# Mixing keys and values of two batches in wide matmuls, with the new layout made by DMA through DRAM scratch

## The chip, the cores and the metric

The kernel runs on one core of a Trainium2 chip. The metric is the device time of one execution in microseconds (us), the median of three runs. The engines are called PE (TensorE, the matmuls), DVE (VectorE), ACT (ScalarE), POOL (GpSimd) and SP (SyncE, which here only issues transfers). PE writes to PSUM, eight banks of 2 KB per partition; DVE and ACT copy from there to SBUF.

## The reference

There are B = 4 batches, H = 8 heads, S = 768 rows and D = 64 columns. The rows of a head are 8 blocks of C = 96 rows. A small 8x8 matrix P per batch and head, normalised five times over rows and columns, mixes blocks of keys and values. Each block of queries then attends to its own mixed block, and the result goes through a gated feed-forward layer.

```
for _ in range(5):
    P = exp(P - max(P, -1)); P = P / sum(P, -1); P = P / sum(P, -2)
k_sorted = einsum('bhij,bhjcd->bhicd', P, k_blocks)
v_sorted = einsum('bhij,bhjcd->bhicd', P, v_blocks)
attn = softmax(q_blocks @ k_sorted^T / 8) @ v_sorted       # within one block of 96
x = attn as (B*S, H*D)                                      # 3072 x 512
out = (silu(x @ w_gate) * (x @ w_val)) @ w_out              # d_ff = 1536
```

## The kernel before, in words

Keys and values lie in SBUF in natural form: partition = (head, block), or (batch in the pair, head, block) for batches 2 and 3 together, and per partition 96 rows of 64 columns, in bf16. `rmix` is a block-diagonal matrix of the P's. The one for batches 2 and 3, `rmix["p"]`, is 128 x 128.

**Mixing and turning in one step.** Scores need keys with D on the partitions, and the product with V needs values with the 96 rows of a block on the partitions. A small matmul does both: the natural data is the stationary operand and `rmix` is the moving one, so the output comes out transposed. `kq_chunk` (line 227) does this for keys, one matmul for each row c and each of two half-arrays (128 x 64 stationary, 64 columns moving). A chunk of 16 rows is 32 matmuls into a pair of PSUM banks, which DVE or ACT then copies to the tile `kqt`. For batches 0 and 1 the other half of the same matmuls turns the queries. For batches 2 and 3 both halves are keys, and the queries go another way: POOL casts them by DMA to DRAM scratch `q_scr` (`q_cast`, line 341), and SP brings them back with a transposing DMA (`q_dma`, line 345). `v_pair_chunk` (line 252) is the same for the values of batches 2 and 3, one matmul of 128 columns for each d. It reads `vch`, a copy of the values ordered (d, c), which POOL makes in four steps (`copy_v`, line 114). Its output is copied to `vt`, whose rows hold D values and a one.

**Attention.** A unit is four blocks of two heads. `scores` makes 8 matmuls, `exps` one exponential on ACT, `av` 8 matmuls with `vt`; DVE takes the reciprocal of the sums and multiplies (tile `st`). The turn of `st` into `xt`, the input of the feed-forward layer, is done either by four PE transposes and a DVE copy (`xtr`) or by a transposing DMA from SP (`x_dma`).

**Feed-forward.** There are eight stages ffn(0) to ffn(7), each of 384 rows of x: 12 gate groups and 12 value groups of 4 matmuls of 384 columns, and the output layer of the stage before in three tiles of three parts, 4 matmuls of 512 columns each. Gate goes to PSUM, ACT takes its tanh, DVE combines both to `gs_sb`; value goes to PSUM and DVE multiplies it with `gs_sb` to `h`.

**PSUM.** Gates, values and some output tiles share three banks ("gen"). One bank ("x") is for transposes and other output tiles. Two pairs of banks ("a" and "b") serve scores, av and the mixing chunks in turn.

**Order.** PE and POOL follow the order in which the program is written. `merge` (line 542) places side work among the groups of a stage: each group counts 0.65 and each output part 0.87, and a side item comes behind the first group at which the sum reaches its number. These numbers are about us of feed-forward work, without the side work. DVE, ACT and SP are ordered by a planner that works with estimated times; each queue then runs in order. In this version the stages that matter are:

```
    merge(ffn(2), units(1, range(4, 8), (0.0, 5.5)) + kqs("p", (13.0, 16.2, 19.4))
          + [(13.0, lambda: q_dma(2)), (16.4, lambda: q_dma(3))])
    merge(ffn(3), vs(v_pair_chunk, 8, [1.15 * n for n in range(8)]) + units(2, range(4), (9.8, 14.0)))
```

`units(2, range(4), ...)` in ffn(3) is the first work that needs mixed keys and values of batches 2 and 3. What `units(b, half)` makes is the input of the feed-forward stage behind it.

## Time and profile before

| | |
|---|---|
| median of three runs (lowest to highest) | 250.45 us (250.2 to 250.91) |
| profiled execution: own time, span | 250.3 us, 248.3 us |
| granted clock of PE | 1.0 |
| busy: PE, DVE, ACT, POOL | 237.2, 157.4, 110.2, 52.5 us |
| stage ffn(2): start and end of its PE work | 77.82 to 107.20 us |
| stage ffn(3) | 107.20 to 136.89 us |
| key mixing for batches 2 and 3, PE (64 matmuls each) | at 93.2, 97.7 and 102.2 us |
| value mixing for batches 2 and 3, PE (8 matmuls each) | eight steps, 107.9 to 119.2 us |
| first scores of batch 2 | 121.3 us |
| the two casts of Q, issued by POOL | at 48.3 and 50.4 us |
| the two transposes of Q, issued by SP | at 85.7 and 92.4 us |

The span runs from the first to the last recorded instruction; the execution's own time has some 2 us around it. A matmul's recorded duration overlaps that of the next one, so the cost of a matmul on PE is read from the distance between starts. A line number such as L236 is a line of the kernel before.

### The profile page before, as it was taken

How to read it: one execution, taken by the hardware profiler on the slowest of the kernel's cores; microseconds unless marked ns; L12 is line 12 of the kernel's file. 1: busy time of each engine (PE TensorE's matmuls, PEld its weight loads, DVE VectorE, ACT ScalarE, POOL GpSimd, SP SyncE). 2: the span in 40 equal slices, each digit the busy share in tenths (PEclk: the TensorE clock that was granted, in tenths of full speed). 3: DMA queues.
4: the chain of work that ended last, by engine and by line, in shares of the span. 5: the costliest groups of instructions: out<-in, count | busy, mean ns of one | idle time of the engine just before them, and what ended most of it. 6: DMA issues, size and time to landing. Idle time of an engine off the chain costs nothing.

```text
span 248.3 us, 6023 instructions
## 1 busy us (share of the span) xinstructions
PE 237.2 (96%) x2552; PEld 141.9 (57%) x2552; DVE 157.4 (63%) x332; ACT 110.2 (44%) x188; POOL 52.5 (21%) x47
## 2 busy tenths in 40 slices
PE   5688999999999999999999999999999999999995
PEld 5375566665565556666655655565555565555543
DVE  6777689785665775857657647755764585446700
ACT  3967543454444444445642552354244334232311
POOL 7938459960059300000000000000000000000000
PEclk9999999999999999999999999999999999999999
DMA  5949999999999299010112121112111111100122
GB/s 101 210 85 171 218 186 225 197 227 216 223 162 194 53 187 156 36 42 3 42 44 64 49 70 32 44 45 74 35 43 42 37 57 57 45 18 26 42 83 89
DMA packets 39530, 24.38 MB, mean 98 GB/s; under 512 B 27728, under 2 KB 35664, under 8 KB 38992
## 3 DMA queue, kind: packets, MB, share of 16 engines
q0 software_dynamic: 21328, 14.16, 38.8%
q1 hardware_dynamic: 18176, 9.84, 15.1%
q8 instruction: 20, 0.33, 0.6%
q14 instruction: 6, 0.05, 0.1%
HBM read 28.32 MB, written 7.86 MB: 146 GB/s over the span
## 4 chain that ended last, share of the span: by engine, by line
PE 85%; DVE 6%; ACT 3%; issue 3%; DMA 2%; DVEq 0%; ACTq 0%; POOLq 0%
PE v_ps L375 24%; PE g_ps L357 23%; PE o_ps L392 23%; PE av_ps L306 3%; PE tkq L236 3%; PE qk L279 3%; DMA v<-in_v_dram 2%; PE tv L258 1%; DVE gs_sb L367 1%; PE tv L248 1%; DVE st L312 1%; PE o_ps L408 1%; ACT e_all L292 1%; DVE h L380 1%; PE x_ps L323 1%
## 5 line engine op out<-in xcount | busy, mean ns | idle before, releaser
L367 DVE SCALAR_TENSOR_TENSOR gs_sb<-th_sb,g_ps 128x384 bf16<-128x384 bf16 x96 | 52.8, 550 | 54.1 <-ACT th_sb L365 51.8
L375 PE MATMUL v_ps<-xt,wv_sb 128*128 128x384 bf16 x380 | 77.5, 326 | 0.5 <-issue 0.2
L357 PE MATMUL g_ps<-xt,wg_sb 128*128 128x384 bf16 x376 | 76.5, 325 | 0.0
L365 ACT ACTIVATE th_sb<-g_ps 128x384 bf16<-128x384 f32 x96 | 47.0, 490 | 57.3 <-PE g_ps L357 54.8
L392 PE MATMUL o_ps<-wo_sb,h 128*128 128x512 bf16 x276 | 64.5, 379 | 0.0
L380 DVE SCALAR_TENSOR_TENSOR h<-v_ps,gs_sb 128x384 bf16<-128x384 f32 x96 | 53.3, 555 | 6.5
L375 PEld LDWEIGHTS <-wv_sb 128*128 128x128 bf16 x380 | 35.7, 97 | 24.5 <-issue 1.8
L357 PEld LDWEIGHTS <-wg_sb 128*128 128x128 bf16 x376 | 34.5, 97 | 22.6 <-issue 0.2
L392 PEld LDWEIGHTS <-h 128*128 128x128 bf16 x276 | 26.1, 98 | 28.3 <-DMA wo_sb<-in_moe_w_out_dram 0.3
L397 ACT COPY o_sb<-o_ps 128x512 f32<-128x512 f32 x23 | 13.4, 585 | 48.7 <-PE o_ps L392 48.7
L122 POOL COPY vch<-v 64x1536 bf16<-64x1536 bf16 (+2 forms) x11 | 28.7, 2648 | 20.4 <-DMA v<-in_v_dram 20.4
L292 ACT ACTIVATE e_all<-qk 96x768 bf16<-96x768 f32 x30 | 22.5, 802 | 9.9 <-PE qk L279 9.9
L312 DVE TENSOR_TENSOR st<-av_ps,r_sb 96x512 bf16<-96x512 f32 x32 | 21.7, 679 | 0.2
L306 PEld LDWEIGHTS <-e_all 96*128 96x128 bf16 x256 | 12.2, 98 | 5.0 <-ACT e_all L292 0.9
L306 PE MATMUL av_ps<-vt,e_all 96*128 96x65 bf16 x256 | 13.5, 194 | 0.2 <-ACT e_all L292 0.2
L216 ACT CAST vt<-tv 96x1024 bf16<-96x1024 f32 (+1 forms) x9 | 9.1, 1027 | 3.7 <-PE tv L258 2.6
L310 DVE RECIPROCAL r_sb<-av_ps 96x8 f32<-96x8 f32 x32 | 6.4, 198 | 7.0 <-PE av_ps L306 7.0
L214 DVE CAST vt<-tv 96x1024 bf16<-96x1024 f32 (+1 forms) x9 | 9.8, 1100 | 1.0 <-PE tv L248 1.0
L214 DVE CAST kqt<-tkq 128x1024 bf16<-128x1024 f32 (+1 forms) x7 | 7.4, 1067 | 3.5 <-PE tkq L236 3.4
L236 PE MATMUL tkq<-rmix,kq 128*64 128x64 bf16 x384 | 7.6, 197 | 1.4 <-issue 0.9
L236 PEld LDWEIGHTS <-kq 128*64 128x64 bf16 x384 | 6.7, 113 | 3.0 <-issue 2.9
L216 ACT CAST kqt<-tkq 128x1024 bf16<-128x1024 f32 (+1 forms) x7 | 6.0, 894 | 5.4 <-PE tkq L236 5.4
(77 smaller groups left out, 127.7 us busy)
## 6 DMA issues: line engine op xcount, KB each, us to landing
out_dram<-o_sb SPq DMA_DIRECT2D x23, 256.0 KB, 2.0
v<-in_v_dram POOLq DMA_DIRECT2D x3, 768.0 KB, 19.8
kq<-in_q_dram POOLq DMA_DIRECT2D x2, 768.0 KB, 13.5
wg_sb<-in_moe_w_gate_dram POOLq DMA_DIRECT2D x6, 256.0 KB, 8.2
wv_sb<-in_moe_w_val_dram POOLq DMA_DIRECT2D x6, 256.0 KB, 9.1
wo_sb<-in_moe_w_out_dram POOLq DMA_DIRECT2D x1, 1536.0 KB, 24.4
kp<-in_k_dram POOLq DMA_DIRECT2D x2, 768.0 KB, 15.1
q_scr<-in_q_dram POOLq DMA_DIRECT2D x2, 768.0 KB, 30.1
```

The costliest lines, as they stand in the source:

```text
L122: eng.tensor_copy(dst, src.transpose([0, 2, 1]))
L214: nc.vector.tensor_copy(dst, src)
L236: nc.tensor.matmul(tp[two * D:(two + 1) * D, lc, :], lhsT=kq_tiles[b][:, at + lc, :], rhs=rm[:, two], start=True, stop=True)
L292: nc.scalar.activation(e_all[:, n:n + 2, 0:4 * C], wide[0:C, :, 0:4 * C], AF.Exp, scale=scale)
L306: nc.tensor.matmul(o[:, two, i4, :], lhsT=e[:, i4 * C:i4 * C + 128], rhs=vt[:, 2 * g + two, half * 4 + i4, :], start=True, stop=True)
L312: nc.vector.tensor_tensor(st.rearrange("p i two d -> p two i d"), o[0:C, :, :, 0:D], r_sb.to_broadcast([C, 2, 4, D]), op=ALU.mult)
L357: nc.tensor.matmul(g_ps, lhsT=wg_sb[:, kc, ts(m, 128)], rhs=xt[:, kc, :], start=(kc == 0), stop=(kc == NKC - 1))
L365: nc.scalar.activation(th_sb, g_ps, AF.Tanh, scale=0.5)
L367: nc.vector.scalar_tensor_tensor(gs_sb, th_sb, 1.0, g_ps, op0=ALU.add, op1=ALU.mult)
L375: nc.tensor.matmul(v_ps, lhsT=wv_sb[:, kc, ts(m, 128)], rhs=xt[:, kc, :], start=(kc == 0), stop=(kc == NKC - 1))
L380: nc.vector.scalar_tensor_tensor(h_tiles[n][:, m, :], v_ps, 0.5, gs_tiles.pop(m), op0=ALU.mult, op1=ALU.mult)
L392: nc.tensor.matmul(o_ps, lhsT=h_w[:, m, ts(t3, 128)], rhs=wo_sb[:, m, :], start=(m == 0), stop=(m == NFC - 1))
```

## The change

Batches 2 and 3 no longer mix and turn in one step. `nat_chunk` takes `rmix["p"]` as the stationary operand and 512 columns of the natural keys or values as the moving one. Twelve such matmuls make all mixed keys of both batches, and twelve all mixed values, still in natural form. Each chunk of 1024 columns is copied to SBUF, keys to a tile `kmix`, values into `vch`.

The new layout is made by DMA. For keys, POOL stores each batch to `k_scr`, with rows (block, c) and columns (head, d), in pieces of 64 elements; SP then loads it with a transposing DMA, as it does the queries (`k_dma`). For values, `v_relay` stores a third of the rows c of all 128 partitions to `v_scr` and loads them back with c on the partitions, one load for each batch, in pieces of 64 elements; both come from POOL. Values need `vch` in the order (d, c) no longer, so the four POOL copies of the pair go.

The side work of ffn(2) and ffn(3) is arranged anew: the keys are mixed first in ffn(2), then the second half of batch 1's attention runs, with the values' mixing in between; ffn(3) has only transfers and the attention of batch 2. The second half of batch 1 turns its result by PE and DVE, as the first half does, and no longer by transposing DMAs. `kqt_tile("q")` is asked for ahead of the tile for keys.

```diff
+    k_scr = [dram.tile([S, H * D], BF16, name=f"k_scr{b}") for b in range(2, B)]
+    v_scr = dram.tile([128, C, D], BF16, name="v_scr")
...
-    def v_pair_chunk(pair, at, n, eng, tag):
...
+    mixed = {}
+
+    def nat_chunk(what, at, eng, tag):
+        src = (kq_tiles["p"] if what == "k" else v_tiles[1]).rearrange("p c d -> p (c d)")
+        if what not in mixed:
+            mixed[what] = (natp.tile([128, C * D], BF16, name="kmix", tag="nat") if what == "k"
+                           else vch[:, 0:C * D])
+        tp = pair_tile("tn", tag)
+        for part in range(2):
+            nc.tensor.matmul(tp[:, part * 512:(part + 1) * 512],
+                             lhsT=rmix["p"].rearrange("p u h i -> p (u h i)"),
+                             rhs=src[:, at + part * 512:at + (part + 1) * 512], start=True, stop=True)
+        drain(eng, mixed[what][:, at:at + 1024], tp)
+
+    def k_out(b):
+        nc.gpsimd.dma_start(
+            out=k_scr[b - 2].rearrange("(i c) (h d) -> h i c d", c=C, d=D),
+            in_=mixed["k"][(b - 2) * R:(b - 1) * R].rearrange("p (c d) -> p c d", d=D))
+
+    def k_dma(b):
+        dst = kqt_tile("p")[:, (b - 2) * GI * C:(b - 1) * GI * C]
+        nc.sync.dma_start_transpose(out=dst.rearrange("p (g s) -> p g s", g=H2), in_=k_scr[b - 2])
+
+    def v_relay(c0, c1):
+        nc.gpsimd.dma_start(out=v_scr[:, c0:c1],
+                            in_=mixed["v"].rearrange("p (c d) -> p c d", d=D)[:, c0:c1])
+        for u in range(2):
+            nc.gpsimd.dma_start(out=vt_tile(1)[c0:c1, u, :, 0:D],
+                                in_=v_scr[u * R:(u + 1) * R, c0:c1].rearrange("n c d -> c n d"))
...
-                if b == 0 or b == 1 and u < H2:
+                if b < 2:
                     todo.append((at + t, lambda w=w, tag=tag: av(b, w, tag)))
                     todo.append((at + t + 3.1, lambda w=w: drain("v", *xtr(b, w))))
...
-    for s in range(4):
-        copy_v(nc.gpsimd, 1, both, s)
-    nc.vector.memset(kqt_tile("p")[:, 2 * GI * C:], 0.0)
-    merge(ffn(2), units(1, range(4, 8), (0.0, 5.5)) + kqs("p", (13.0, 16.2, 19.4))
-          + [(13.0, lambda: q_dma(2)), (16.4, lambda: q_dma(3))])
-    merge(ffn(3), vs(v_pair_chunk, 8, [1.15 * n for n in range(8)]) + units(2, range(4), (9.8, 14.0)))
+    def nats(what, ats, engs):
+        return [(at, lambda m=m: nat_chunk(what, m * 1024, engs[m], "ba"[m % 2])) for m, at in enumerate(ats)]
+
+    kqt_tile("q")
+    merge(ffn(2), nats("k", (0.0, 1.2, 2.4, 3.6, 4.8, 6.0), "vssvss")
+          + [(6.1, lambda: (k_out(2), k_out(3)))] + units(1, range(4, 8), (7.0, 13.3))
+          + nats("v", (11.7, 12.0, 16.8, 18.2, 19.0, 20.0), "svssvs")
+          + [(12.1, lambda: v_relay(0, 32)), (18.3, lambda: v_relay(32, 64)), (20.1, lambda: v_relay(64, 96))]
+          + [(13.0, lambda: q_dma(2)), (22.0, lambda: (nc.vector.memset(kqt_tile("p")[:, 2 * GI * C:], 0.0), k_dma(2)))])
+    merge(ffn(3), [(1.0, lambda: q_dma(3)), (6.0, lambda: k_dma(3))] + units(2, range(4), (11.0, 15.5)))
```

## The prediction

> **What bounds the kernel now.** I read the engine totals and the 40 slices first, to learn which engine has no slack and whether transfers are short where the change lies:
>
> ```profile
> span 248.3 us, 6023 instructions
> ...
> PE 237.2 (96%) x2552; PEld 141.9 (57%) x2552; DVE 157.4 (63%) x332; ACT 110.2 (44%) x188; POOL 52.5 (21%) x47
> ...
> DMA  5949999999999299010112121112111111100122
> ...
> PE 85%; DVE 6%; ACT 3%; issue 3%; DMA 2%; DVEq 0%; ACTq 0%; POOLq 0%
> ```
>
> PE (TensorE) is busy nearly throughout and carries 85% of the chain that ended last. The transfers are heavy in slices 0 to 12 and 14 to 15 (one slice is 6.2 us) and light behind. Next, the busy time of each engine in the two stages that the diff rewrites, ffn(2) and ffn(3):
>
> ```profile
> 77.82:107.20 29.38, 29.38 (x389) 17.52 (x388) 19.25 (x35) 13.45 (x22) 4.73 (x2) 1.00 0.73 109
> 107.20:136.89 29.69, 29.54 (x261) 18.09 (x260) 19.96 (x36) 14.77 (x23) 0.00 (x0) 1.00 0.14 41
> ```
>
> The columns are length, then PE, weight loads, DVE, ACT, POOL, clock, DMA share, GB/s. PE is full, DVE has a third free, ACT half. So a removed PE step is worth its spacing in the chain, as long as DVE and ACT return the PSUM banks in time. The spacings come from the chain, in order of time (start, us, what):
>
> ```profile
> 76.95 0.17 PE x_ps L323 x4
> ...
> 92.60 0.65 PE v_ps L375 x4
> 93.25 1.13 PE tkq L236 x64
> 94.38 2.70 PE o_ps L392 x12
> ...
> 98.86 0.76 PE v_ps L375 x4
> ...
> 104.78 2.59 PE o_ps L392 x12
> ...
> 108.02 0.45 PE tv L258 x8
> ...
> 123.05 0.50 ACT th_sb L365
> 123.56 0.56 DVE gs_sb L367
> ...
> 126.57 0.70 DVE st L312
> ```
>
> The reader should see two things. The small matmuls are cheap: 64 of them take 1.13 us, 18 ns each, although each is recorded at 197 ns. And the few places where the chain leaves PE are all near the exponentials: a tanh that stood behind two of them, and the normalised tile `st`. Last, the transfers that resemble the new ones (issuing queue, count, size, median us to landing):
>
> ```profile
> q_scr<-in_q_dram POOLq DMA_DIRECT2D x2, 768.0 KB, 30.1
> xt<-st SPq DMA_TRANSPOSE x20, 2.3
> kqtq<-q_scr SPq DMA_TRANSPOSE x2, 7.0
> ```
>
> **What the Trainium skill says.** "TensorE: Matmul & The Clock Gate", Step-by-step: back-to-back matmuls of 512 columns follow each other about every 216 ns. The trace agrees: 12 in 2.59 us is 0.216. "DMA: Bandwidth & Descriptors", Anatomy of one DMA (SWDGE): a transfer from POOL costs about 2 us plus its bytes; the trace shows no such transfer alone, but SP's stores land in 2.0. The same page, Why a DMA increments its semaphore by 16: a transfer runs on as many engines, up to 16, as divide the slowest dimension of both sides. The store of the mixed keys has heads (8) outermost, so I expect 8 engines; no row of before has such a shape. The same page, Two DMAs through the same engine are not ordered: a read of scratch must wait for the write's completion, so each relay is two trips in series. The trace of before has no such pair at the place of need.
>
> **The change, on PE.** Removed: 3 key steps of 64 matmuls, 3 x 1.13 = 3.39, and what each costs the group behind it (2.70 for 2.59, 0.76 for 0.65), 3 x 0.11 = 0.33; 8 value steps of 8 matmuls, 8 x 0.45 = 3.6. Together 7.3 us. Added: 24 matmuls of 512 columns, 24 x 0.216 = 5.2; and the second half of batch 1 is turned by PE again, 4 groups x 0.175 (the x_ps row) = 0.7. Together 5.9. Net on PE: -1.4 us.
>
> The two stages hold 0.7 us of PE waits now: 0.13 in ffn(2), 0.55 in ffn(3), found by adding the parts (0.65 a gate or value, 0.864 an output part, 0.55 a score pair, 0.26 an av, and the steps above) and comparing with 29.38 and 29.69. If they went and none came, PE would gain 2.1. That is the most the change can give.
>
> **On DVE and ACT.** Removed: 7 copies out of PSUM on each (DVE 1.22, ACT 1.01 to 1.19). Added: 12 of the same 128x1024 size, 4 on DVE, 8 on ACT, taken at the same 1.2 and 1.0 since only the output's stride changes; and 4 copies of turned tiles on DVE (0.35 each). The total falls, but all of it now lies in ffn(2): DVE 19.25 - 3 x 1.22 + 4 x 1.2 + 4 x 0.35 = 21.8 us in a stage of some 32. The margin is in the groups of four gates and values (5.2 us of PE, 8 x 0.555 = 4.4 of DVE), where it is thin. I laid the new order out and followed the banks (three for gate and value, pairs a and b):
> - Gates 0 to 3 with key steps 0 to 4: two ACT copies stand ahead of a tanh each, and each bank returns 0.1 to 0.2 us before its use. Wait 0.1.
> - Gates 4 to 7: the score pair moves from behind a gate to right behind an output group. ACT then has the output copy (0.585) and two exponentials (1.50) ahead of the next tanh. Where before has exponentials ahead of a tanh (123.05 above), PE lost 0.24; with the output copy I take 0.43. Then value step 1 needs pair a back from the second av: DVE owes 6 gate/value operations (3.3), two normalisations (1.76) and that step's copy before the next score pair, and starts late. I take 0.45.
> - Gates 8 to 11: two value steps follow an av or a copy on the same pair within 1.3 to 1.6 us. Wait 0.25.
> - ffn(3): the first score pair is better placed (that tanh goes first), the second again follows an output group: 0.43, and 0.25 behind it.
>
> Sum 1.9 us; if ACT takes the tanh ahead of the second exponential, some 0.9. The first follows what ACT did at 121.65, two exponentials in a row. The gain of 2.1 against waits of 1.9 leaves -0.2 us.
>
> **Moved or hidden steps.** POOL's four reorderings of V (11.2 us, at 71 to 82) go; nobody waited for them, worth 0. The 4 transposes by SP for batch 1 go (2.3 us to landing, not needed until ffn(3)), worth 0 beside the PE cost above; SP's queue gets lighter. The last transpose for ffn(4) is closer: its av now stands 3.9 us before that stage, plus 0.5 until the fourth weight block needs it. Before took 1.55 from av to issue and 2.3 to landing. Slack 0.5, cost 0; uncovered, up to 1 us.
>
> Keys: the six copies end at about 88. Two stores of 6144 pieces of 128 B follow. The casts of Q, of as many pieces, ended at about 81 and took some 5.7 us each (69.5 to 81 for two); POOL issued each in 3.2. Bounds: 5 us, or 11 each on 8 engines. Landed by 100 to 113. SP's transpose of batch 2 takes 7.0, so 107 to 120, and batch 2's scores start at 121.6 (layout 120.3 and waits). The 7.0-us transpose of batch 3 has until ffn(5). Behind the waiting transposes on SP stand output stores, one per 9 us with three buffers: no wait.
> Values: the third relay can start at 108.5. Its write (512 KB, some 4.6 us with the fixed part) ends at 113; two reads of 2048 pieces of 128 B, into rows of 130 B, are issued in about 1 us each and take 1.3 to 4 us each plus 2: landed at 118 to 124. The first av is at 124. POOL waits on each write with only the next relay behind it. I take these as hidden; the cover is 1 to 9 us.
>
> Buffers: Q^T now takes the tile of batch 0, free at the start of ffn(2), so its first transpose (85.7 before) can start sooner; K^T takes batch 1's, free after the score pair at 97. The 32-column fill before K^T is one DVE memset (0.1). Worth 0.
>
> Span 248.3 - 0.2 = 248.1. The profiled run took 250.3, 2.0 around its span and 0.15 below the median of 250.45; on the median's scale, 250.2.
>
> **Rivals.** (A, forecast) PE's saving is given back in waits for PSUM banks: 250.2, own range 249.5 to 251.
> (B) The saving comes through: tanh goes first and copies fit in DVE's idle time. Speaking for it: DVE idles over 2 us in each output group, and eight value copies in ffn(3) now cost PE nothing. Waits 0.5: -1.6, 248.8. Against it: the third of DVE that is free lies mostly in those output groups.
> (C) Slower: the relays are late at batch 2's first av. Decides once a relay takes more than 15.5 us from its last copy (108.5) to landing (124). If small pieces at odd rows and three transposes at once make it 18, PE stops 2.5 us: 252.7. For it: the Q casts were 30 us from issue to landing in a full queue. Against: the queue is light from 100 on, at 46 GB/s in the last third of ffn(2).
> (D) The waits of A come to twice the size: 3.8 - 2.1 = +1.7, 252.1.
>
> **Numbers.** A 0.52, B 0.25, C 0.13, D 0.10. A measurement of this kernel can't tell less than about 0.3% (0.75 us) from no change. Faster than 249.7: nearly all of B and a fifth of A, 0.34. Slower than 251.2: C, most of D and a little of A, 0.24. The same: 0.42. The range 248.7 to 252.3 leaves out the better half of B and most of C; it is the span of the unknown waits (0.4 to 3.9).
>
> **What would show it.** PE: 24 matmuls of `tn` spaced 0.216, stage ffn(2) at 32.0 to 33 us, ffn(3) at 26 to 27. A shows as value or gate groups spaced by more than 0.65 near score pairs, with DVE or ACT in the chain there; B as none of these; C as the first score pair or av of batch 2 waiting for a DMA. It fails if the wide matmuls are not spaced 0.216, or the planner orders ACT or SP otherwise.

## The result: slower by 16%, and the profile after

| | before | after |
|---|---|---|
| median on one chip, four runs each (lowest to highest) | 250.68 us (250.2 to 251.84) | 291.87 us (289.0 to 293.11) |
| ratio after / before, 95% interval | | 1.1619 [1.1522, 1.1716] |
| profiled execution: own time, span | 250.3, 248.3 us | 289.0, 287.2 us |
| stage ffn(2) | 77.82 to 107.20 | 77.62 to 110.82 |

Here and below, a ratio leaves out the executions in a slower state of the chip, while a median and a range in brackets take in all of them. The forecast of 250.2 was wrong, and its range too. What came is the rival that was given 0.13, the late relay, at fifteen times its size. The page of the kernel after, totals and slices (one slice is 7.2 us):

```profile
span 287.2 us, 5583 instructions
...
PE 238.0 (83%) x2311; PEld 139.2 (48%) x2336; DVE 155.9 (54%) x333; ACT 110.5 (38%) x189; POOL 57.2 (20%) x54
...
PE   5889999999999999930000599999999999999995
...
PEclk9999999999999999995555599999999999999999
DMA  6979999999994758869595612211112012100102
...
PE 53%; DMA 31%; DVE 5%; POOL 5%; issue 4%; ACT 1%; POOLq 0%; DVEq 0%; ACTq 0%
```

PE is as busy in all as before (238.0 against 237.2 us). There is one hole, slices 18 to 22, and DMA now carries 31% of the chain that ended last, where it carried 2%. The waits of the kernel after name the hole (engine, what waits, for what: total, times, longest):

```profile
PE av_ps L328 <- DMA vt<-v_scr: 36.5, 1, 36.5
```

One wait, 36.5 us, at batch 2's first av. The rest of the span's growth of 38.9 us is small: PE's timeline of the kernel after shows that PE comes back at half clock,

```profile
161.14 0.60 PE L328 MATMUL av_ps<-vt,e_all 96*128 96x65 bf16 x8 [36.51 <-DMA vt<-v_scr]
161.96 3.19 PE L414 MATMUL o_ps<-wo_sb,h 128*128 128x512 bf16 x7 [0.22 <-issue]
164.95 0.65 PE L328 MATMUL av_ps<-vt,e_all 96*128 96x65 bf16 x8
```

seven matmuls of 512 columns in the 2.99 us between two starts, where 7 x 0.216 is 1.5: 1.5 us more. The steps around them are slowed too. Stage ffn(3) takes 64.89 us (110.82 to 175.71), so 28.35 without the wait; in e15 below, where no transfer is late, it takes 26.04. These 2.3 us are nearly all of the rest. The Trainium skill ("TensorE: Matmul & The Clock Gate", Part 1: The HAM clock gate) says that after it has been idle PE runs at half its clock for about the first 3.4 us of work, and that this varies from run to run. The trace shows the half clock too, but for longer, some 4.5 us: that follows from the mean granted clock of 0.54 in the 4.86 us from 161.14 on (the columns are those of the windows in the prediction; the clock stands third from the end).

```profile
161.14:166.00 4.86, 4.64 (x26) 2.34 (x28) 1.23 (x4) 0.00 (x0) 0.00 (x0) 0.54 0.23 30
```

The prediction priced a wait for its length alone. Where the 36.5 us come from is in POOL's timeline of the kernel after (start, length of the issue, instruction, idle before and its releaser):

```profile
88.72 3.85 POOL L269 DMA_DIRECT2D k_scr<-kmix  x1 [34.61 <-ACT kmix L218]
108.45 3.83 POOL L269 DMA_DIRECT2D k_scr<-kmix  x1 [15.88 <-DVE vch L216]
112.20 0.67 POOL L278 DMA_DIRECT2D v_scr<-vch  x1
129.29 2.15 POOL L281 DMA_DIRECT2D vt<-v_scr  x2 [16.42 <-DMA v_scr<-vch]
131.42 0.57 POOL L278 DMA_DIRECT2D v_scr<-vch  x1
142.21 2.11 POOL L281 DMA_DIRECT2D vt<-v_scr  x2 [10.21 <-DMA v_scr<-vch]
144.31 0.57 POOL L278 DMA_DIRECT2D v_scr<-vch  x1
153.83 2.11 POOL L281 DMA_DIRECT2D vt<-v_scr  x2 [8.95 <-DMA v_scr<-vch]
```

Two stores of keys, then three relays, each a write and two reads. The second store comes out of POOL only at 108.45, when the first has landed (it takes some 19 us). The first write of values stands behind it, so it leaves at 112.2, although the second copy that it needs, on DVE, ended at 97.9. Then each write is waited for before its reads, and each later write stands behind the reads before it: 16.4, 10.2 and 9.0 us. The last read lands at 161.0; the av is ready at 124.6.

What a write waits for in that time can be seen in the trace's records of single packets of 4 KB, which no view here shows; the length of a packet tells which transfer it belongs to. From 145 to 150, behind the third write's issue, packets of about 1 us are under way, sixteen at a time, as in the third relay's reads alone (157 to 161). The write's own packets, most of them of 0.16 us, come at 151 and 152. So most of that wait is the reads issued just ahead of the write on POOL's queue. In the same way the packets of the first write come at 125 and 126, behind those of the second store.

The sizes, from the list of transfers of the kernel after (queue, count, size, median us to landing):

```profile
k_scr<-kmix POOLq DMA_DIRECT2D x2, 768.0 KB, 19.2
v_scr<-vch POOLq DMA_DIRECT2D x3, 512.0 KB, 10.5
vt<-v_scr POOLq DMA_DIRECT2D x6, 256.0 KB, 9.0
kqtp<-k_scr SPq DMA_TRANSPOSE x2, 7.6
```

The prediction had 5 to 11 for the first row, 4.6 for the second, 3.3 to 6 for the third.

### The profile page after: what moved, and what is told of

It reads as the page before. It is cut to its first block, busy times and chain, and to the rows that moved or that the text cites. A ratio compares the mean times of both kernels' runs of the same rounds, so it can differ in the third digit from the quotient of the medians.

```text
span 287.2 us, 5583 instructions
## 1 busy us (share of the span) xinstructions
PE 238.0 (83%) x2311; PEld 139.2 (48%) x2336; DVE 155.9 (54%) x333; ACT 110.5 (38%) x189; POOL 57.2 (20%) x54
## 4 chain that ended last, share of the span: by engine, by line
PE 53%; DMA 31%; DVE 5%; POOL 5%; issue 4%; ACT 1%; POOLq 0%; DVEq 0%; ACTq 0%
PE o_ps L414 19%; PE v_ps L397 14%; PE g_ps L379 13%; DMA v_scr<-vch 13%; DMA wo_sb<-in_moe_w_out_dram 8%; DMA kq<-in_k_dram 4%; DMA wv_sb<-in_moe_w_val_dram 4%; DMA vt<-v_scr 2%; PE av_ps L328 2%; DVE gs_sb L389 2%; PE qk L301 2%; DVE h L402 1%; POOL k_scr L269 1%; POOL wg_sb L111 1%; PE tn L263 1%
## 5 line engine op out<-in xcount | busy, mean ns | idle before, releaser
L414 PE MATMUL o_ps<-wo_sb,h 128*128 128x512 bf16 x257 | 63.3, 386 | 1.9 <-DVE h L402 0.4
L419 ACT COPY o_sb<-o_ps 128x512 f32<-128x512 f32 x23 | 13.5, 587 | 92.5 <-PE o_ps L414 92.5
L328 PE MATMUL av_ps<-vt,e_all 96*128 96x65 bf16 x256 | 13.9, 197 | 36.9 <-DMA vt<-v_scr 36.5
L414 PEld LDWEIGHTS <-h 128*128 128x128 bf16 x276 | 26.8, 99 | 30.8 <-issue 2.4
L124 POOL COPY vch<-v 64x1536 bf16<-64x1536 bf16 (+1 forms) x7 | 17.5, 2539 | 2.6 <-DMA v<-in_v_dram 2.6
L269 POOL DMA_DIRECT2D k_scr<-kmix x2 | 7.7, 3841 | 50.5 <-ACT kmix L218 34.6
L281 POOL DMA_DIRECT2D vt<-v_scr x6 | 6.4, 1067 | 35.6 <-DMA v_scr<-vch 35.6
## 6 DMA issues: line engine op xcount, KB each, us to landing
kp<-in_k_dram POOLq DMA_DIRECT2D x2, 768.0 KB, 14.7
```

Of the source, the lines that this page charges most:

```text
L124: eng.tensor_copy(dst, src.transpose([0, 2, 1]))
L328: nc.tensor.matmul(o[:, two, i4, :], lhsT=e[:, i4 * C:i4 * C + 128], rhs=vt[:, 2 * g + two, half * 4 + i4, :], start=True, stop=True)
L414: nc.tensor.matmul(o_ps, lhsT=h_w[:, m, ts(t3, 128)], rhs=wo_sb[:, m, :], start=(m == 0), stop=(m == NFC - 1))
L419: nc.scalar.copy(o_sb, o_ps)
```

## The experiments

In the order in which they were run. A kernel's times stand beside runs of the kernel before on the same chip (median 251.04 to 251.39 us). Where a time is of one run only, what is read from it is its profile, or a difference of several us.

### One half of the change alone

Keys by the new way, values by the old small matmuls (e1_k_only), and the reverse (e2_v_only). At this point two theories stood: that the stores of keys, spread over few engines and ahead in POOL's queue, hold the relays up; and that the relays are late by themselves.

```diff
# e1_k_only: values mixed by small matmuls in ffn(3), as before
-          + nats("v", (11.7, 12.0, 16.8, 18.2, 19.0, 20.0), "svssvs")
-          + [(12.1, lambda: v_relay(0, 32)), (18.3, lambda: v_relay(32, 64)), (20.1, lambda: v_relay(64, 96))]
-    merge(ffn(3), [(1.0, lambda: q_dma(3)), (6.0, lambda: k_dma(3))] + units(2, range(4), (11.0, 15.5)))
+    merge(ffn(3), [(1.0, lambda: q_dma(3)), (6.0, lambda: k_dma(3))] + vs(v_pair_chunk, 8, [1.15 * n for n in range(8)])
+          + units(2, range(4), (9.8, 14.0)))
```
```diff
# e2_v_only: keys mixed by small matmuls at the start of ffn(2)
-    merge(ffn(2), nats("k", (0.0, 1.2, 2.4, 3.6, 4.8, 6.0), "vssvss")
-          + [(6.1, lambda: (k_out(2), k_out(3)))] + units(1, range(4, 8), (7.0, 13.3))
+    merge(ffn(2), kqs("p", (0.0, 2.4, 4.8)) + units(1, range(4, 8), (7.0, 13.3))
...
-    merge(ffn(3), [(1.0, lambda: q_dma(3)), (6.0, lambda: k_dma(3))] + units(2, range(4), (11.0, 15.5)))
+    merge(ffn(3), [(1.0, lambda: q_dma(3))] + units(2, range(4), (11.0, 15.5)))
```

> Keys mixed wide and relaid by DMA as in the change; values as in the kernel before (POOL's four reorderings, eight small-matmul steps in ffn(3)). Theory 1 (the value relays, pushed back behind the key stores on POOL, are the whole loss): the first store lands near 108, the transpose at 116, the first scores of batch 2 need it at 121, so PE waits for no transfer. On PE: -3.7 for the key steps, +2.6 for twelve wide matmuls, +0.7 for the turns by PE, so about -0.4 plus up to 1 us of bank waits: 249.5 to 251.5. Rival (the key path alone is late as well): PE waits at the first scores, 254 or more.

> Values mixed wide and relayed as in the change; keys by small matmuls as in the kernel before (in the place of the wide key steps), so no key stores and no key transposes. Theory 1 in its plain form (only the key stores in front hold the relays up): the first relay's write starts near 97, the third relay has landed by 124, PE waits for nothing: 250 to 252. Rival, theory 2 (three relays in series are too long by themselves, some 12 us each as they show when they run one after the other at 131 to 161): the third lands near 130 to 133, PE waits 6 to 9 us at the first av of batch 2: 256 to 260.

e1: 255.47 us (254.71 to 258.66), ratio 1.0177 [1.0107, 1.0247]. Two stages take 29.92 and 30.75 us where before took 29.38 and 29.69. No score waits for keys, so the time is in the rival's range without the rival's wait. In these stages the trace names two larger waits of PE, 1.0 and 0.5 us, and the chain leads from both to SP: the transpose of batch 3's keys is issued at 128.99 and the four transposes of x queue behind it. That is 1.6 us of the 4.9 by which this profile's span is longer than before's. Another 2.1 lie ahead of ffn(2), which starts at 79.93 here, with waits of 0.65 and 1.35 us for weights at 41.9 and 44.1; the last 1.2 lie behind and were not traced. POOL's timeline of e1 has nothing but the two stores:

```profile
91.04 3.84 POOL L279 DMA_DIRECT2D k_scr<-kmix  x1 [6.24 <-ACT kmix L218]
110.40 3.83 POOL L279 DMA_DIRECT2D k_scr<-kmix  x1 [15.52 <-issue]
```

The second store waits 15.5 us with nothing ahead of it on POOL but the first.

e2: 271.2 us. Without any store of keys PE still waits 18.1 us for `vt`. So the stores are not all of it: both expectations were under. The second write and SP's second transpose of Q took some 17 us each in the same stretch of time, where a write alone took 4 (POOL's and SP's timelines of e2):

```profile
103.79 2.13 POOL L281 DMA_DIRECT2D vt<-v_scr  x2 [3.83 <-DMA v_scr<-vch]
106.83 0.57 POOL L278 DMA_DIRECT2D v_scr<-vch  x1 [0.91 <-ACT vch L218]
124.28 2.10 POOL L281 DMA_DIRECT2D vt<-v_scr  x2 [16.88 <-DMA v_scr<-vch]
```
```profile
104.56 17.41 SPq L369 DMA_TRANSPOSE kqtq<-q_scr  x1
```

By the packet records it is again the reads ahead of the write, those of the first relay, that share the engines with the transpose: from 106 to 121 the packets on POOL's queue take up to 4.6 us each, and some hundred of 0.16 us, the write's, follow at 122 and 123.

### The stores off POOL's queue, or over more engines

```diff
# e3_k_from_sp
-        nc.gpsimd.dma_start(
+        nc.sync.dma_start(
             out=k_scr[b - 2].rearrange("(i c) (h d) -> h i c d", c=C, d=D),
```
```diff
# e4_k_64_rows: 64 partitions outermost, same pieces of 128 B
-            out=k_scr[b - 2].rearrange("(i c) (h d) -> h i c d", c=C, d=D),
+            out=k_scr[b - 2].rearrange("s e -> (s e)").rearrange("(c p d) -> p c d", c=C, d=D),
```

> The changed kernel with the two key stores issued from SP and not from POOL; nothing else. Theory 1: POOL is free when the first values are copied, the first relay starts near 97 and not at 112, and what remains is theory 2's length of the relays beside the stores: PE waits 10 to 22 us and not 36.5, time 264 to 276. Rival (POOL isn't held up, the 16 DMA engines are short): the relays are as late as before, 285 to 292.

> The changed kernel with another order in the key scratch: the outermost dimension of the store is the 64 partitions on both sides, the pieces are 128 B as before (rows 8 KB apart). The keys of batches 2 and 3 that come back are in a wrong order, the work is the same. If the number of DMA engines (8 heads outermost, so 8 of 16) makes the store slow and fills POOL's queue: the store takes 10 us or less in place of 19, the second is issued right behind the first and not when it has landed, the first relay starts near 97, time 262 to 276. Rival (pieces of 128 B into DRAM are slow whatever the shape): the store takes 15 us or more and the time stays at 283 to 292.

e3: 283.0 us. The first write leaves at 99.83 instead of 112.20, so the block on POOL was real. But the lateness went to SP's queue: PE waits 17.1 us for the keys at the scores, 5.3 behind an output copy on ACT whose buffer waits for an output store (SP's queue again), and 3.4 for `vt`. e4: 280.36 us, PE waits 25.3 us for `vt`; both stores leave POOL in a row, in 4.37 us, and take 14.7 us to landing each. Both times lie between the two ranges expected: the places were right and the gains too small. The windows while the stores ran (length, then PE, weight loads, DVE, ACT, POOL, clock, DMA share, GB/s), e3 and then e4:

```profile
91.00:96.00 5.00, 4.72 (x41) 2.88 (x40) 3.37 (x9) 2.48 (x5) 0.00 (x0) 1.00 0.46 65
```
```profile
96.00:101.00 5.00, 4.68 (x45) 2.56 (x44) 4.55 (x11) 1.92 (x4) 0.32 (x1) 1.00 0.99 112
```

With 8 heads outermost the stores move 65 GB/s, with 64 partitions outermost 112. The share of 0.46 looks like half of the engines, but it belongs to the stores issued by SP. In the kernel after, where POOL issues the same store, the window shows

```profile
92.50:105.00 12.50, 12.05 (x103) 6.82 (x104) 9.79 (x21) 6.28 (x10) 0.07 (x1) 1.00 0.70 59
```

a share of 0.70 at 59 GB/s, so the share alone doesn't count engines. The packet records do: in the kernel after eight packets of 4 KB are under way at a time (the median from 94 to 104; nine at most), in e4 sixteen, and they take 0.56 and 0.54 us each. Nor is the cause how far apart the pieces lie in DRAM: 1 KB apart in the kernel after, but 8 KB in e4 and 256 B in e13 below, whose store also has sixteen packets under way. That is the prediction's count of engines, with its price: in the kernel after, 6144 pieces on 8 engines are 768 for each, in about 14.5 us (92.5 to 107), 19 ns a piece. Yet each of these two cures alone gave back only 9 to 12 us: the relays stayed slow.

### Pieces made large

Here I formed a third theory: pieces of 128 B are the cause, because together they are more work than the DMA engines can do before the first av. Large pieces for all (e5_all_large), for keys alone (e6_keys_large), for the reads of values alone (e7_values_large):

```diff
# keys (e5, e6): a partition's row as one piece, in the wrong order
-            out=k_scr[b - 2].rearrange("(i c) (h d) -> h i c d", c=C, d=D),
-            in_=mixed["k"][(b - 2) * R:(b - 1) * R].rearrange("p (c d) -> p c d", d=D))
+        nc.gpsimd.dma_start(out=k_scr[b - 2].rearrange("s e -> (s e)").rearrange("(p f) -> p f", p=R),
+                            in_=mixed["k"][(b - 2) * R:(b - 1) * R])
# reads of values (e5, e7): 4 KB pieces, the column of ones overwritten
-            nc.gpsimd.dma_start(out=vt_tile(1)[c0:c1, u, :, 0:D],
-                                in_=v_scr[u * R:(u + 1) * R, c0:c1].rearrange("n c d -> c n d"))
+            nc.gpsimd.dma_start(out=vt_tile(1)[c0:c1, u].rearrange("c n e -> c (n e)")[:, 0:R * D].rearrange("c (two f) -> c two f", two=2),
+                                in_=v_scr[u * R:(u + 1) * R, c0:c1].rearrange("(p two) c d -> p two (c d)", two=2))
```

> The changed kernel with the same transfers, bytes and waits, but no small pieces: the key stores write 12 KB rows, the relay's reads move 4 KB pieces. The keys and values that come back are in a wrong order and the ones in the value tile are overwritten. Theory 3 (pieces of 128 B are the cause: about 18 to 23 ns each on a DMA engine, 24576 of them, together more engine time than there is before batch 2's first av): no wait for a transfer, stage ffn(2) 32 to 33.5 us, 249.5 to 253. Rival (two trips in series, three relays one behind the other, whatever the pieces): PE waits 5 us or more at the first av, 256 and up.

> Only the key stores write 12 KB rows (the keys come back in a wrong order); the value relays are those of the change. Theory 3: both stores have landed by 97 and no longer hold POOL's queue; the relays alone take some 36 us from 97 to 133, PE waits 8 to 12 us at the first av, 259 to 263. Rival (the relays also lose to the key and query transposes on SP, as in the kernel with new values only, where a transpose took 17 us to issue): PE waits 15 us or more, 266 to 272.

> Only the relay's reads move 4 KB pieces (values in a wrong order, ones overwritten); the key stores are those of the change. The second key store is still queued only when the first has landed, near 108, and the first relay's write stands behind it until 127. Then each relay is short, some 7 us: the third has landed near 146, PE waits 17 to 24 us, 270 to 278. If the relays' reads were the larger part of the loss, the wait would be under 12 us.

e5: 259.71 us (257.65 to 260.96), ratio 1.0337 [1.0259, 1.0415], PE waits 5.8 us for `vt`. That is in the rival's range (a wait of 5 us or more), so pieces are not the whole cause. e7: 275.55 us, as expected, PE waits 21.9. e6: 277.66 us, above both of its expectations, PE waits 24.9. POOL's timeline of e6:

```profile
98.71 0.56 POOL L277 DMA_DIRECT2D v_scr<-vch  x1 [8.97 <-issue]
103.44 2.15 POOL L280 DMA_DIRECT2D vt<-v_scr  x2 [4.17 <-DMA v_scr<-vch]
106.20 0.57 POOL L277 DMA_DIRECT2D v_scr<-vch  x1 [0.61 <-ACT vch L218]
130.44 2.11 POOL L280 DMA_DIRECT2D vt<-v_scr  x2 [23.67 <-DMA v_scr<-vch]
```

The first write leaves 13 us earlier than in the kernel after and lands in 4. The second then takes 24: ahead of it stand the first relay's small reads, and beside them run both transposes of keys, which are no longer held back by the stores. Time taken from one place came back in another. Small pieces are the main price (36.5 us of waiting against 5.8), but no part of them alone. So the third theory was widened: what counts is the sum of what the DMA engines have to do before the first av, and the order of POOL's queue decides which part of it stands ahead.

### The row of 130 bytes

```diff
# e8_rows_160: rows of the value tile 160 B apart, the same pieces
-            t = vtp.tile([C, 2, H * NB, D + 1], BF16, name=f"vt{pair}", tag="vt")
+            t = vtp.tile([C, 2, H * NB, D + 16], BF16, name=f"vt{pair}", tag="vt")[:, :, :, 0:D + 1]
```

> The changed kernel with rows of the value tile 160 B apart and not 130 B, so that every piece of 128 B starts at a multiple of 32 B. If the odd start makes the relay's reads slow: the last two reads land in 5 us or less and not in 7.2, and the time falls by 4 to 8 us. Rival (the number of pieces counts, not where they start): 7 us again, and 286 to 293.

281.06 us; PE waits 28.0 us instead of 36.5. The reads' median falls from 9.0 to 5.3 us, with nothing changed but where a row starts:

```profile
vt<-v_scr POOLq DMA_DIRECT2D x6, 256.0 KB, 5.3
```

The wait fell by 8.5 us, where 4 to 8 of the time were expected. The waits for the second and third write fell as well, from 10.2 and 9.0 us to 6.9 and 5.0, though nothing of the writes was changed: they stand behind the reads. The prediction mentioned "rows of 130 B" and gave them no price.

### One cure after the other

The next three test theory 3, as widened, by taking work from ahead of the first av. e9_all_large_late is e5 with batch 3's store and transpose of keys, which nobody needs before ffn(5), moved to ffn(4). e10_rows_late does the same with small pieces and the wide rows of e8. e12_rows_late_64 adds the store of e4.

```diff
# e9, e10, e12
-          + [(6.1, lambda: (k_out(2), k_out(3)))] + units(1, range(4, 8), (7.0, 13.3))
+          + [(6.1, lambda: k_out(2))] + units(1, range(4, 8), (7.0, 13.3))
...
-    merge(ffn(3), [(1.0, lambda: q_dma(3)), (6.0, lambda: k_dma(3))] + units(2, range(4), (11.0, 15.5)))
-    merge(ffn(4), units(2, range(4, 8), (0.0, 8.0)))
+    merge(ffn(3), [(1.0, lambda: q_dma(3))] + units(2, range(4), (11.0, 15.5)))
+    merge(ffn(4), units(2, range(4, 8), (0.0, 8.0)) + [(0.5, lambda: k_out(3)), (1.0, lambda: k_dma(3))])
```

> The run with all transfers in large pieces (keys in the wrong order, the column of ones overwritten, a tiny extra fill), and batch 3's store and transpose of keys moved from ffn(2)/ffn(3) to ffn(4), behind the value relays. Theory 3 (the sum of what the DMA engines have to do before the first av decides, and the order of POOL's queue decides what of it stands ahead): ahead of the first av are now one store of keys, three transposes and three relays; the relays land some 4 to 6 us earlier than in the run with all transfers large, PE waits 0 to 2 us for vt, and what is left is the change on PE, DVE and ACT alone: 250.5 to 253, ffn(2) at 32.5 to 33.5. Rival (the relays need their own time in series whatever is beside them, and a relay of large pieces takes 10 us): PE still waits 4 us or more, 256 to 260.

> The kernel after with rows of the value tile 160 B apart, and batch 3's store and transpose of keys moved to ffn(4), behind the relays; all pieces still 128 B; nothing left out. Theory 3: the first write is issued at about 103 instead of 112, since no second store blocks POOL, and batch 3's transpose no longer lies beside the relays; of the 28 us that the run with the wide rows waited, 9 go with the store and a few with the transpose: PE waits 13 to 19 us for vt, time 264 to 272. Rival (the relays' own small reads alone are what is late, and the store ahead of them only fills time in which they'd wait for one another): PE waits 22 us or more, 274 to 282.

> As the run with wide rows and the late store, and the one store of keys that is left has 64 partitions outermost (pieces still 128 B, keys in the wrong order), so that it spreads over all 16 engines: it lands some 7 us earlier. Theory 3: the relays start at 100 to 101 and PE waits 8 to 15 us, 259 to 267, 2 to 6 us below the run with 8 engines. Rival (after the first store is through, nothing of it is left on the path: the third value copy at 108 and the relays in series behind it decide): within 2 us of the run with 8 engines.

e9: 251.31 us (249.84 to 254.47, 20 runs) against 251.09, ratio 1.0011 [0.9987, 1.0036]; no wait for a transfer; theory 3 held and its rival fell. e10: 271.37 us. PE waits 8.1 us for `vt`, and 7.9 for `xt` at the next stage, whose transposes now run beside batch 3's late store: 16.0 in all; the 13 to 19 us expected were for `vt` alone. The time is in the expected range. e12: 250.42 us in one run, below both expectations; no wait for a transfer at all. The direction is theory 3's, the size neither theory's. POOL's timelines, e10 and then e12, show why the store's engines were worth so much:

```profile
99.62 0.57 POOL L278 DMA_DIRECT2D v_scr<-vch  x1 [5.92 <-issue]
110.96 2.14 POOL L281 DMA_DIRECT2D vt<-v_scr  x2 [10.77 <-DMA v_scr<-vch]
...
128.48 2.11 POOL L281 DMA_DIRECT2D vt<-v_scr  x2 [5.00 <-DMA v_scr<-vch]
```
```profile
98.60 0.59 POOL L278 DMA_DIRECT2D v_scr<-vch  x1 [7.59 <-issue]
102.83 2.12 POOL L281 DMA_DIRECT2D vt<-v_scr  x2 [3.64 <-DMA v_scr<-vch]
...
119.60 2.11 POOL L281 DMA_DIRECT2D vt<-v_scr  x2 [5.22 <-DMA v_scr<-vch]
```

POOL's wait for the first write is 10.8 us behind the rest of the 8-engine store and 3.6 without it. That 7 us, and 1 us of earlier start, go through the series of relays: the last reads leave 8.9 us earlier, just in time, and the late `xt` goes with them. So the wait falls in steps, 36.5 (after), 28.0 (wide rows), 16.0 (late store), 0 (16 engines). No single cause owns it; the order in which they are taken away sets the share that each seems to have.

### The whole change with its transfers off the path

e12's keys are in the wrong order. e13_heads_apart puts them right: the mixed keys leave the matmul ordered (half of the head pair, head pair, block), and a store then has one even stride over 32 partitions. It also puts the second and third write ahead of their reads.

```diff
+    rmix_k = const.tile([128, 128], BF16, name="rmix_k")
...
-    k_scr = [dram.tile([S, H * D], BF16, name=f"k_scr{b}") for b in range(2, B)]
+    k_scr = [dram.tile([H2, S, 2 * D], BF16, name=f"k_scr{b}") for b in range(2, B)]
...
+                for u in range(2):
+                    nc.vector.tensor_copy(rmix_k[:, u * R:(u + 1) * R].rearrange("p (e g i) -> p e g i", e=2, i=NB),
+                                          rmix["p"][:, u].rearrange("p (g e) i -> p e g i", e=2))
...
+        for e in range(2):
+            nc.gpsimd.dma_start(
+                out=k_scr[b - 2].rearrange("g (i c) (e d) -> e (g i) c d", c=C, e=2)[e],
+                in_=mixed["k"][lo + e * R // 2:lo + (e + 1) * R // 2].rearrange("p (c d) -> p c d", d=D))
...
-        nc.sync.dma_start_transpose(out=dst.rearrange("p (g s) -> p g s", g=H2), in_=k_scr[b - 2])
+        nc.sync.dma_start_transpose(out=dst, in_=k_scr[b - 2].rearrange("g s x -> (g s) x"))
```

e14_fewer_bank_waits is e13 with five places of the PE order and of the copies' engines changed, each at a PE wait for a PSUM bank:

```diff
-    merge(ffn(2), nats("k", (0.0, 1.2, 2.4, 3.6, 4.8, 6.0), "vssvss")
-          + [(6.1, lambda: k_out(2))] + units(1, range(4, 8), (7.0, 13.3))
-          + nats("v", (11.7, 12.0, 16.8, 18.2, 19.0, 20.0), "svssvs")
+    merge(ffn(2), nats("k", (0.0, 1.2, 2.4, 3.6, 4.8, 5.1), "vssssv")
+          + [(6.1, lambda: k_out(2))] + units(1, range(4, 8), (7.0, 13.3), (0.1, 0.0))
+          + nats("v", (11.7, 12.5, 16.8, 18.2, 19.0, 20.0), "svssvs")
...
-    merge(ffn(3), [(1.0, lambda: q_dma(3))] + units(2, range(4), (11.0, 15.5)))
+    merge(ffn(3), [(1.0, lambda: q_dma(3))] + units(2, range(4), (11.0, 15.5), (0.0, 0.8)))
```

(The added pair of numbers moves a score pair forward by so much.)

> A whole kernel with the transfers rearranged: rows of the value tile 160 B apart; batch 3's keys stored and transposed in ffn(4); the mixed keys leave the matmul ordered (half of the head pair, head pair, block) instead of (head, block), by a permuted copy of the mixing matrix, so that two stores of 32 partitions each have one even stride outermost and can spread over 16 engines with the keys in the right order; the second and third write of values stand ahead of the second and third read in POOL's queue. Theory 3: as with the rows 160 B apart, the late store and 64 partitions outermost (250.4): no wait for a transfer at the first av, the stages ffn(2) and ffn(3) together at 59.3 to 59.8 us, and the time within 0.4% of before, 249.8 to 251.8, since the saving of PE is used up by waits for PSUM banks. Rival (32 partitions in a store are as slow as 8 outermost dimensions): the first store takes 18 us again, PE waits 5 us or more, 256 to 265.

> The run before in this call, with five places in the order changed and nothing else: the sixth key step stands ahead of the first output part instead of behind it; the fourth key copy goes to ACT and the sixth to DVE; two score pairs stand ahead of the last output part of their stage instead of behind it; the second value step and its write come 0.65 us later. Each is at one of the four PE waits of 0.25 to 0.43 us seen in ffn(2) and ffn(3), together 1.3. Theory A of the prediction (what PE saves is given back in waits for PSUM banks): ffn(2) and ffn(3) get shorter by 0.6 to 1.3 us, 249.2 to 250.2, 0.2 to 0.5% below the run before. Rival (the waits only move to the next bank, since DVE and ACT are what is short): the same within 0.2%.

e13: 259.2 us (258.59 to 263.75), ratio 1.0305 [1.028, 1.033]; 249.8 to 251.8 was expected. No wait at the first av, and ffn(2) with ffn(3) take 59.23 us, but a new wait stands at batch 3's first scores. PE's timeline of e13:

```profile
153.61 0.26 PE L310 MATMUL qk<-kqtq,kqtp 64*128 64x96 bf16 x2 [5.75 <-DMA kqtp<-k_scr]
```

and SP's:

```profile
142.21 3.31 SPq L369 DMA_TRANSPOSE xt<-st  x2
...
147.88 3.59 SPq L282 DMA_TRANSPOSE kqtp<-k_scr  x1
```

The keys had left POOL at 117.5 to 120; the planner put their transpose behind two of x, which wait for PE's own work.

e14: 257.4 us, ratio 1.0232 [1.0194, 1.0271]. Two edits took away the waits of 0.43 and 0.30 us (first output part, first value group behind the exponentials) and left nothing in their place. The others made new ones, 0.90 and 0.75, where 0.32 and 0.25 had been: a score pair now stood where its bank was still being copied. ffn(2) and ffn(3) together took 59.31, no less than in e13, so theory A's claim for this run fell and its rival's words fit: the waits moved. The whole-kernel difference to e13 is the shorter wait for batch 3's keys (3.5 us).

Two runs for these two points. In e15_sp_in_order SP's queue follows the program, with the keys' transpose ahead of the four of x; e16_two_waits is e15 with only the two good edits of e14.

```diff
# e15, against e13
-    man = tc.manual_schedule(engines={ET.PE, ET.Pool})
+    man = tc.manual_schedule(engines={ET.PE, ET.Pool, ET.SP})
...
-          + [(13.0, lambda: q_dma(2)), (22.0, lambda: (nc.vector.memset(kqt_tile("p")[:, 2 * GI * C:], 0.0), k_dma(2)))])
-    merge(ffn(3), [(1.0, lambda: q_dma(3))] + units(2, range(4), (11.0, 15.5)))
+          + [(0.1, lambda: q_dma(2)), (4.0, lambda: q_dma(3)), (14.1, lambda: (nc.vector.memset(kqt_tile("p")[:, 2 * GI * C:], 0.0), k_dma(2)))])
+    merge(ffn(3), units(2, range(4), (11.0, 15.5)))
```
```diff
# e16, against e15
-    merge(ffn(2), nats("k", (0.0, 1.2, 2.4, 3.6, 4.8, 6.0), "vssvss")
-          + [(6.1, lambda: k_out(2))] + units(1, range(4, 8), (7.0, 13.3))
+    merge(ffn(2), nats("k", (0.0, 1.2, 2.4, 3.6, 4.8, 5.1), "vssssv")
+          + [(6.1, lambda: k_out(2))] + units(1, range(4, 8), (7.0, 13.3), (0.1, 0.0))
```

> As the run with the heads apart, but SP's queue follows the order of the program from ffn(0) on, with the transposes of Q at the start of ffn(2) and the one of batch 3's keys at the start of ffn(4), ahead of the four transposes of x there instead of behind two of them. If the 5.8 us that PE waited for batch 3's keys at 147.4 were a matter of place in SP's queue (that transpose was issued at 147.9, 30 us after its data had been stored), the wait goes, no other transfer is late, and the time is 250.3 to 252, within 0.4% of before. If the transpose is late for its data or for the DMA engines, PE still waits 3 us or more, 254 or more.

> The run beside it in this call, with two of the five edits for the bank waits kept: the sixth key step ahead of the first output part (fourth key copy on ACT, sixth on DVE), and batch 1's score pair ahead of the last output part of the first half of ffn(2). These took away waits of 0.43 and 0.30 us without leaving new ones; the other edits had put 0.90 and 0.75 in the place of 0.32 and 0.25. Theory A: ffn(2) and ffn(3) together 0.5 to 0.8 us shorter than in the run beside it, 0.2 to 0.3% less time, and at or just below the kernel before: 249.8 to 251.2. Rival (each wait taken away comes back one bank later): no shorter than the run beside it.

e15: 251.61 us (249.89 to 253.79, 22 runs) against 251.29, ratio 1.0011 [0.999, 1.0032]. The wait for keys is gone, so it was a place in SP's queue. e16: 249.85 us (248.31 to 251.56, 22 runs), ratio 0.9944 [0.9923, 0.9965]: faster than the kernel before, by 0.6%, measured on one chip, and the only version here that is shown to beat both. The two stages in windows, e15 and then e16 (columns as before):

```profile
77.47:110.64 33.17, 31.88 (x233) 17.46 (x236) 21.51 (x41) 17.99 (x27) 6.45 (x7) 1.00 1.05 188
110.64:136.68 26.04, 25.63 (x194) 14.50 (x196) 16.08 (x32) 10.30 (x19) 6.87 (x6) 1.00 0.63 128
```
```profile
77.30:109.05 31.75, 31.46 (x233) 17.39 (x236) 21.53 (x41) 17.89 (x27) 6.45 (x7) 1.00 1.13 200
109.05:135.09 26.04, 25.63 (x194) 14.49 (x196) 16.09 (x32) 10.30 (x19) 6.86 (x6) 1.00 0.61 127
```

Together 59.21 and 57.79 us, where before has 59.07. DVE and ACT do the same amount of work in both; its order differs, and two copies have changed places between them. That alone is worth 1.4 us. That is above the 0.5 to 0.8 expected: the wait of 0.32 at the second value step went too. In ffn(2) of e16 the timeline of PE names no wait on DVE or ACT.

## Why the prediction was wrong, and where it was right

**The step that failed** is "Moved or hidden steps": "I take these as hidden; the cover is 1 to 9 us". Its mechanism of failure was the prediction's own rival C. Its terms were mis-sized one by one:

- *A store of keys*, "5 us, or 11 each on 8 engines": 19.2. The count of 8 engines was right, as the Trainium skill has it ("DMA: Bandwidth & Descriptors", Why a DMA increments its semaphore by 16), and the trace agrees with eight packets under way at a time. But the price came from the casts of Q, 5.7 us for 6144 pieces, by doubling. If the Q casts use 16 engines, they cost 15 ns a piece on each (5.7 us / 384); the store cost 19, and its fixed parts come on top.
- *Two stores in one queue.* "Landed by 100 to 113" has room for two stores one after the other; they landed at 108 and 127. What it left out is that the second leaves POOL only when the first has landed, and that the write of values stands behind it: 112.2 instead of 99.8 (e3). "POOL waits on each write with only the next relay behind it" left out what stood ahead. Moving that store and its transpose, which nobody needed until ffn(5), took 12 us (28.0 of waiting in e8, 16.0 in e10).
- *A write*, 4.6: about 4 with little beside it (the first writes of e2, e6 and e12), right. With other transfers ahead of it in POOL's queue or beside it, 9 to 24. The prediction let the third write start at its own last copy and so left out the reads of the relay before, which the packet records show ahead of the write. It added up the landings, but not the work of the transfers: two stores, two transposes of 6 to 7 us, three relays.
- *A read*, 3.3 to 6: 9.0 with rows of 130 B, 5.3 with rows of 160 B. The row's start was the part without a price.
- *The queue is light, at 46 GB/s.* That was the kernel before. GB/s is also the wrong measure for small pieces: the stores keep their eight engines busy at 59 to 65 GB/s.

Rival C itself had the right place (batch 2's first av, its bar being a relay longer than 15.5 us from 108.5) and put the relay at 18 us. The last relay landed 52.5 us after 108.5. The chance of 0.13 came from judging each transfer by its own length.

**What held.** The wide matmuls are spaced 0.216: two in 0.43 (from 79.48 to 79.91 in e12, and so throughout). ffn(2) took 33.20 us in the kernel after, just above the forecast of 32.0 to 33. ffn(3), once no transfer is late, 26.04, forecast 26 to 27. No score of batch 2 waits for keys. The half of the forecast that PE's saving is given back in waits for PSUM banks, -0.2 us net, came out at +0.14 (59.21 in e15 against 59.07). By the prediction's own parts, 59.07 - 0.7 of waits - 1.4 saved is 56.97 without waits, so e15 has 2.2 us of them (forecast 1.9), and e16 0.8. The windows say the same: PE is busy for 57.51 of the 59.21 us in e15, where before it was 58.92 of 59.07, so 1.4 us of work are saved, as forecast, and 1.5 us of idle time added. The places were near those named: 0.43 at the first output part (0.1 forecast there), 0.30 at a tanh behind two exponentials (0.43), 0.32 at the second value step (0.45), 0.25 in ffn(3) (0.25). Of the six waits forecast two did not come, one in each stage, so the sum agrees better than its parts. e16 is case B, the saving that comes through, found by moving two score and key steps. That its gain over e15 comes from these steps and copies is shown by the two runs, which differ in nothing else; three of the four waits are gone.

**What stays open.** Nothing the second store needs was missing until 108.45: it reads the same six copies as the first. The profile names DVE in the kernel after and "issue" in e1, both only by coincidence in time. That the queue can hold no more descriptors for 8 engines is inferred: with 16 engines both stores left at once (e4, 4.37 us). How a transpose and small reads slow each other (17 us in e2, 24 in e6) was seen, not taken apart. The last five runs change several things against the kernel after; what each is worth by itself was measured only along one order of taking them away.

## What to carry to other kernels

A relayout moved from PE to DMA is priced by pieces and by engines, not bytes: count the pieces that each engine gets, add up all transfers that lie before the first consumer, and walk through the issuing queue in order, since a transfer that nobody needs yet delays all that stand behind it. Put what is needed first at the head, issue a write ahead of reads that would hold it up (as e13 does), give a store a slowest dimension that spreads over all engines (32 or 64 here, not 8), and try another pitch for small rows (160 B here, not 130). And before an engine's saved time is called a gain, see whether the steps around it can take it up: here the same work in another order was worth 1.4 us.

## What the runs showed of the hardware that I had not expected

- Reads of 128-byte pieces into rows 130 B apart land in 9.0 us, into rows 160 B apart in 5.3 (medians of six, after and e8).
- A store with 8 heads outermost has eight packets under way and moves 59 to 65 GB/s (after, e3), one with 64 partitions outermost sixteen and 112 (e4). POOL did not issue a second store of the first kind until the first had landed, 15 to 16 us with POOL idle (after, e1).
- A write issued by POOL right behind small reads waits for them: most of its own packets take 0.16 us each, but it lands 10.8 and 9.5 us after its issue (the second and third write of after), and sooner when only the reads are made faster (e8).
- A 768 KB transpose of 6 to 7 us took up to 17 us beside small reads of values, and the write behind these as long, where it takes 4 alone (e2).
- In e2 the stores of keys were gone and the wait fell only from 36.5 to 18.1 us; in e6 they were made cheap, and it fell only to 24.9, since the transposes and small reads that they had held apart now met.
